# Constant matmuls into spare score columns where the planner sees TensorE idle, with new keys for the first part

## The chip, the cores and the metric

The kernel runs on one core of a Trainium2 chip. The metric is the time of one execution on the device in microseconds (us). Before the change the median of three runs is 1089.22 us (1087.53 to 1090.05). The profile is of one further execution, whose own time is 1085.3 us; its span, from the first to the last instruction, is 1083.5 us.

## What is computed

Attention over 4 batches, 8 heads, 576 positions and a head width of 64, in which each row keeps only the scores within `tau` of its maximum, then two feed-forward layers of 2304 tokens, width 512 and hidden width 2048:

```python
scores = scale * np.matmul(q, k.transpose(0, 1, 3, 2))
thresh = np.max(scores, axis=-1, keepdims=True) - tau
scores = np.where(scores >= thresh, scores, -1000000000.0)
scores = scores - np.max(scores, axis=-1, keepdims=True)
attn = np.exp(scores)
attn = attn / (np.sum(attn, axis=-1, keepdims=True) + 1e-09)
x = np.matmul(attn, v)                  # heads joined: 2304 x 512
h = x @ w_in;  x = (h * np.clip(h + 3.0, 0.0, 6.0) / 6.0) @ w_out
h = x @ w2_in; x = (h - np.tanh(h)) @ w2_out
```

## The kernel before

**Numbers in pairs.** To keep float32 accuracy on TensorE (PE), operands are split into a high and a low part and multiplied in three passes (`mm3`, L502). The weights arrive as 64-bit values and are put together by shifts and masks on VectorE (DVE; L432, L435, L438).

**Units of attention.** `units` lists 144 units, each one block of 128 queries of one head (or the left-over queries of two heads). `softmax(u)` makes the scores of a unit on PE (L692: four matmuls of 288 columns, or eight for the left-over queries, 640 in all) into a PSUM tile `s` of two banks, of which each uses 288 of its 512 columns (`ps.t[:, :, 0:SH]`). Three readers follow: the maximum on DVE (L697), the exponential on ScalarE (ACT, L699), and on DVE the comparison with the threshold, multiplied by the exponential (L708). There are two such tiles (`R_s`), so unit u+2 waits for L708 of unit u. The weights of attention are then split (L713 on ACT, L719 on GpSimd, POOL), transposed by a DMA (`pt`), and multiplied with the values (`products`, L745, 28 matmuls of 65 columns for each block).

**The first feed-forward layer** has two halves of the hidden width and eight blocks of tokens. Ten passes (`PASSES`, `layer1`) run beside attention: 12 matmuls of `m<-xT,wo` (L502) for each of 8 hidden tiles, 96 in a pass, and 96 of `m<-g,wo` (L933). Six more passes (`ENDING`) follow, and then the second layer. Its weights need a scale first (`weights_done`: L995 on PE, L1000 to L1016 on DVE), and each block of tokens too (`x_scale`, `x_round`: L482, L489, L827 on PE, L832 on DVE).

**What sets the order.** All work is recorded as tasks by `plan.add(eng, dur, key, fn, ...)`: an engine, a duration, a key, what is read and written. `Plan.issue` then runs a list schedule by these durations: whenever an engine is free, the ready task with the lowest key is issued, and `fn` emits its instructions. So the order of every engine's queue is fixed at build time; on the chip each engine takes its queue in order, and semaphores hold it where a partner is late. The constants `LK, LQ, ...` (how many units ahead keys and queries are transposed), `T0, W0, FO, FW` (when attention, weights and passes are due) and `PVK, GK, RK` (offsets of keys) set the keys. The durations are those of a full TensorE clock: 0.53 us for a unit's scores, 0.404 us for a block's products.

Of the kernel before, what the change touches and what calls it, by code (L numbers as in the profile page):

```python
# [2 lines left out]

# [11 lines left out]
BF16 = mybir.dt.bfloat16  # L15
# [57 lines left out]
class Plan:  # L73
# [8 lines left out]
    SAME = {"pe": 0.0, "act": 0.1, "dve": 0.127, "pool": 0.03, "dma": 0.0, None: 0.0}  # L82

    def __init__(self):
        self.tasks = []

    def add(self, eng, dur, key, fn, r=(), w=(), after=(), xfer=0.0, hold=False, slack=0.0, port=None):
        r, w = ([getattr(b, "of", b) for b in x] for x in (r, w))
# [14 lines left out]
    def issue(self):  # L103
        succ = {t: [] for t in self.tasks}
        left = {}
        for n, t in enumerate(self.tasks):
            t.seq = n
            for b in t.w:
                t.deps.update(dict.fromkeys(b.ring.after))
                if b.prev is not None:  # L110
                    t.deps.update(dict.fromkeys(b.prev.users))
            t.deps.pop(t, None)
            left[t] = len(t.deps)
            for d in t.deps:
                succ[d].append(t)
        engs = ("pe", "act", "dve", "pool", "dma", None)
        free = dict.fromkeys(engs, 0.0)
        pending = {e: [] for e in engs}
        avail = {e: [] for e in engs}
        at = dict.fromkeys(self.tasks, 0.0)  # L120
        for t in self.tasks:
            if not left[t]:
                heapq.heappush(pending[t.eng], (0.0, t.seq, t))
        rings = {b.ring for t in self.tasks for b in t.free}
        slacks = {t.slack for t in self.tasks}
        now, done, moving = 0.0, 0, 0.0
        port = {"dve": 0.0, "pool": 0.0}
        while done < len(self.tasks):
            for e in engs:
                while pending[e] and pending[e][0][0] <= now:  # L130
                    t = heapq.heappop(pending[e])[2]
                    heapq.heappush(avail[e], (t.key, t.seq, t))
                if free[e] > now:
                    continue
                held = []
                while avail[e]:
                    x = heapq.heappop(avail[e])
                    if all(b.slot is not None or b.ring.slot_at(now - x[2].slack) is not None for b in x[2].free):
                        break
                    held.append(x)  # L140
                    x = None
                else:
                    x = None
                for y in held:
                    heapq.heappush(avail[e], y)
                if x is None:
                    continue
                t = x[2]
                for b in t.free:
                    if b.slot is None:  # L150
                        b.slot = b.ring.slot_at(now - t.slack)
                        b.ring.slots[b.slot] = float("inf")
                t.fn()
                t.start = now
                done += 1
                end = free[e] = (max(now, port["pool" if e == "dve" else "dve"]) if t.port else now) + t.dur
                if t.port:
                    port[e] = end
                if t.xfer or e == "dma":
                    end = moving = max(moving, now + 1.3) + t.xfer  # L160
                    if t.hold:
                        free[e] = max(free[e], end - 0.9)
# [12 lines left out]
            nxt = [x + y for r in rings for x in r.slots for y in slacks if now < x + y < float("inf")]  # L175
            for e in engs:
                if free[e] > now and (avail[e] or pending[e]):
                    nxt.append(free[e])
                elif pending[e]:
                    nxt.append(pending[e][0][0])  # L180
            nxt = [x for x in nxt if x > now]
            assert nxt or done == len(self.tasks), "the tasks wait for each other"
            if nxt:
                now = min(nxt)
        return now
# [15 lines left out]
def attention_moe_moe_kernel(  # L201
# [29 lines left out]
    nc = tc.nc  # L231
# [3 lines left out]
    KD = DM // 128  # L235
    FH = DFF // 2
    MH = FH // 128
# [5 lines left out]
    SH = S // 2  # L243
# [11 lines left out]
    plan = Plan()  # L255
# [1 line left out]

    LAG = 4
    STEP, SLOW, KNEE = 3.0, 0.8, 4
    LK, LQ, LV, LD = 5, 3, 1, 4  # L260
    XL, FO = 1, 7
    FW = 38.0
    W0, WS, WO = 8.0, 0.8, -2.0
    PVK, GK, RK = -4.0, -6.0, -1.0
    T2O = 0.0
    PASSES = [(0, 0, 0), (0, 1, 0), (1, 0, 0), (0, 0, 1), (1, 1, 0), (0, 1, 1), (2, 0, 0), (1, 0, 1), (2, 1, 0), (3, 0, 0)]
    CLAMP, LOD = True, (8, 8)
# [4 lines left out]
    F0, EK, CL, P2L, CF = 2.0, 4.0, 0.2, 22.0, 1.0  # L272
    NF, SF, PACE, PREP, PW, TK = 18, 14, 11.0, 2, 55.0, 40
    PK, PREP0 = (100.0, 90.0), 1
    T0 = 12.0
    WB0, WBS, WBD, WBL, WBP = 34, 2, 0.8, 8.0, 3.0
    WAL, WAP = 7.0, 0.8
    ZU, TAIL = 30, 3
    ST, SB, CS = 4.0, 2.0, 0.0


    const = ctx.enter_context(tc.tile_pool(name="const", bufs=1))
# [193 lines left out]
            out=p.bitcast(I32), in0=p.bitcast(I32), scalar1=0x7F800000, scalar2=None, op0=ALU.bitwise_and)  # L476
        nc.vector.reciprocal(out=inv, in_=p)

    def highest(src, top, key, after, ring):

        bank = ring.new()
        x = add("pe", 0.3, key, lambda: nc.tensor.transpose(bank.t[0:1, 0:128], src, ident), w=[bank], after=after)  # L482
        return add("dve", 0.26, key + 0.1, lambda: nc.vector.tensor_reduce(
            out=top, in_=bank.t[0:1, 0:128], axis=AX.X, op=ALU.max), r=[bank], w=[bank], after=[x])

    def everywhere(top, key, after, ring, dur, fn):

        bank = ring.new()
        x = add("pe", 0.1, key + 0.2, lambda: nc.tensor.matmul(  # L489
            bank.t[:, 0:1], ones[0:1, :], top, start=True, stop=True), w=[bank], after=after)  # L490
        return add("dve", dur, key + 0.3, lambda: fn(bank.t[:, 0:1]), r=[bank], w=[bank], after=[x])

    def flat(ap):
# [167 lines left out]
    def queries(b, g, j, h, c, part):  # L661

        if c == NC:
            return QT[b, "l", j].t[:, part, h % 2 * LF:h % 2 * LF + 2 * LF]
        return QT[b, g, j].t[:, part, h % 2, c % 2 * 128:c % 2 * 128 + 128]

    GT, XT = {}, {}

    def sum_group(u):

# [5 lines left out]
    def softmax(u, key):  # L676
# [9 lines left out]
        ex = lambda: e.t[:, n, :].rearrange("p (a s) -> p a s", a=2)  # L686

        def scores():
            ops = [(queries(b, g, j, x, c, part), KS[b, j].t[:, x % 2]) for x in hs for part in range(2)]
            for i, (l, ks) in enumerate(ops):  # L690
                for half in range(2):
                    nc.tensor.matmul(  # L692
                        ps.t[:, half, 0:SH], l, ks[:, half * SH:(half + 1) * SH], start=i == 0, stop=i == len(ops) - 1,
                    )
# [96 lines left out]
    def x_scale(b, g, key):  # L791

        hb = 2 * b + g
        x = add("dve", 0.15, key, lambda: nc.vector.tensor_reduce(
            out=xtop[:, hb:hb + 1], in_=xsq[:, hb, 0:2 + g], axis=AX.X, op=ALU.max), after=x_done[b, g])
        x = highest(xtop[:, hb:hb + 1], one[0:1, hb % 4:hb % 4 + 1], key + 0.1, [x], R_tp)
        x = everywhere(one[0:1, hb % 4:hb % 4 + 1], key + 0.1, [x], R_tp, 0.45, lambda bank: root(
            bank, xpow[:, 0, hb:hb + 1], xpow[:, 1, hb:hb + 1]))
        x_scaled[b, g] = x

    def x_unscale(b, g, half, key):
# [11 lines left out]
    def x_round(b, g, i, key):  # L813
# [12 lines left out]
            for kk in range(KD):  # L826
                nc.tensor.transpose(pv()[:, kk, :], xn()[:, kk * 128:(kk + 1) * 128], ident[0:w, 0:w])  # L827

        add("pe", 0.00085 * KD * w, key, tr, r=[xt], w=[tp, xT], after=[x_scaled[b, g]])
        hi = add("act", t_act(KD * w, scalars=True), key + RK, lambda: nc.scalar.activation(  # L830
            out=xT.t[:, 0, :, cols], in_=pv(), func=ACTF.Copy, scale=s), r=[tp], w=[xT])
        add("dve", t_dve(KD * w, scalars=True), key + RK, lambda: nc.vector.scalar_tensor_tensor(  # L832
# [107 lines left out]
        turn.append(last)  # L940

    with tc.manual_schedule():
        make_identity(nc, ident)
        nc.sync.dma_start(out=tau_b[:, 0:1], in_=tau.partition_broadcast(128))
        nc.vector.tensor_scalar(out=tau_b[:, 1:2], in0=tau_b[:, 0:1], scalar1=0.0, scalar2=None, op0=ALU.max)
# [2 lines left out]
        )  # L948
        nc.vector.tensor_scalar(out=tau_b[:, 3:4], in0=tau_b[:, 1:2], scalar1=-1.0, scalar2=None, op0=ALU.mult)
        nc.vector.memset(three[:, 0:1], 3.0 * GS)  # L950
        nc.vector.memset(ones, 64.0)
        nc.vector.memset(xsq.rearrange("p b i -> p (b i)"), 0.0)
        for t in vt_t:
            for i in range(2):
                nc.gpsimd.memset(t[:, i, :, :, D:D + 1].rearrange("p h c d -> p (h c) d"), 1.0 - i)
# [28 lines left out]
        def weights_done(half, kind, key, step):  # L984
# [12 lines left out]
            x = add("pe", 0.07 * MH * KD, key, norms, r=ss, w=[gram], after=w_found[half, kind])  # L997
# [5 lines left out]
            x = add("dve", 0.5, key, diagonal, r=[gram], w=[gram], after=[x])  # L1003
            bank = R_tp.new()
            x = add("pe", 0.12, key, lambda: nc.tensor.matmul(
                bank.t[:, 0:1], ones, top, start=True, stop=True), w=[bank], after=[x])
# [135 lines left out]
        key = T2  # L1142
# [451 lines left out]
```

## Time and profile before

| | us |
|---|---|
| median of three runs | 1089.22 |
| profiled execution, its own time | 1085.3 |
| its span | 1083.5 |
| PE busy (92% of the span) | 996.8 |
| DVE busy (75%) | 813.5 |
| ACT busy (67%) | 724.5 |
| POOL busy (33%) | 354.7 |

The page cuts the span into 40 slices of 27 us and gives the busy share of each engine in tenths, and the clock that TensorE was granted. A busy share says little by itself; what a stage waits for is read from the views of waits and from the chain of work that ended last, in windows of the stage in question.

### The profile page before, as it was taken

The page shows a single profiled execution, that of the slowest core. Times are in us where ns is not written, and L with a number is a line of the kernel's source. Part 1 is how long each engine was busy: PE and PEld are TensorE (multiplying, and loading weights), DVE is VectorE, ACT ScalarE, POOL GpSimd, SP SyncE. Part 2 cuts the span into 40 slices and gives each one's busy share as a digit, 9 for nine tenths or more (in the row PEclk, how much of TensorE's full clock was granted, in tenths as well). Part 3 has the DMA queues.
Part 4 walks back from the last instruction along what each step waited for, and adds up shares of the span by engine and source line. Part 5 has one row for each costly group of instructions (what it writes and reads, how often), then busy time and mean ns, then how long its engine had stood idle before and what let it go on. Part 6 is the DMA issues. An engine that isn't in the chain of part 4 may idle for free.

```text
span 1083.5 us, 23225 instructions
## 1 busy us (share of the span) xinstructions
PE 996.8 (92%) x8919; PEld 762.9 (70%) x8919; DVE 813.5 (75%) x1625; ACT 724.5 (67%) x1347; POOL 354.7 (33%) x377
## 2 busy tenths in 40 slices
PE   5654987989899999999999999999999999999998
PEld 4553776768788788888786787876576666666664
DVE  5888888979687587877557894478987796784664
ACT  6775877888998688876645874457756675574332
POOL 3553545776775565764310000000001111111000
PEclk8686997999999999999999999999999999999999
DMA  7896689988778667667468744224334866574235
GB/s 185 177 203 173 136 177 209 194 198 158 141 159 170 123 155 171 115 146 159 92 198 266 262 154 121 64 85 139 100 126 124 200 136 115 127 127 51 87 96 138
DMA packets 284943, 161.43 MB, mean 149 GB/s; under 512 B 203168, under 2 KB 261024, under 8 KB 284832
## 3 DMA queue, kind: packets, MB, share of 16 engines
q1 hardware_dynamic: 279024, 150.25, 56.8%
q0 software_dynamic: 5184, 9.44, 6.4%
q8 instruction: 70, 1.15, 0.4%
q14 instruction: 41, 0.34, 0.1%
q10 hardware_dynamic: 624, 0.26, 0.1%
HBM read 76.02 MB, written 41.42 MB: 108 GB/s over the span
## 4 chain that ended last, share of the span: by engine, by line
PE 73%; DVE 10%; ACT 8%; DMA 4%; issue 3%; POOL 1%; SPq 0%; ACTq 0%; DVEq 0%
PE ya L502 23%; PE m L502 19%; PE h L502 9%; PE m L933 7%; PE s L692 6%; PE tp L745 5%; DMA pt<-pp 2%; DVE e L708 2%; PE tp L575 2%; ACT e L699 1%; DMA xT<-xs 1%; DVE z L697 1%; DVE m L435 1%; DVE wo L438 1%; PE tp L827 1%
## 5 line engine op out<-in xcount | busy, mean ns | idle before, releaser
L502 PEld LDWEIGHTS <-wo 128*128 128x128 f16 x2112 | 201.5, 98 | 59.1 <-issue 4.6
L719 POOL TENSOR_TENSOR pp<-e,pp 128x128 f16<-128x128 f32 (+3 forms) x156 | 180.3, 1176 | 115.1 <-ACT pp L713 67.7
L502 PE MATMUL ya<-wo,g 128*128 128x512 f16 x864 | 205.4, 379 | 2.5 <-DVE g L857 1.3
L502 PEld LDWEIGHTS <-wi 128*128 128x128 f16 x1536 | 150.0, 98 | 39.3
L502 PE MATMUL m<-xT,wo 128*128 128x256 f16 (+1 forms) x1248 | 171.8, 286 | 3.9 <-DVE wo L438 3.2
L1414 POOL DMA_DIRECT2D po<-o x36 | 31.3, 876 | 410.5 <-ACT o L1408 410.5
L502 PEld LDWEIGHTS <-g 128*128 128x128 f16 x864 | 83.7, 98 | 82.1 <-DVE g L857 3.1
L708 DVE SCALAR_TENSOR_TENSOR e<-s,z,e 128x576 f32<-128x576 f32 x144 | 116.4, 812 | 30.6 <-ACT e L699 26.5
L933 PE MATMUL m<-g,wo 128*128 128x256 f16 (+1 forms) x960 | 129.4, 284 | 5.3 <-ACT y L878 2.7
L697 DVE TENSOR_REDUCE z<-s 128x1 f32<-128x576 f32 x144 | 107.6, 752 | 34.1 <-PE s L692 33.2
L692 PE MATMUL s<-ks,q 128*128 128x288 f32 x512 | 107.8, 338 | 22.5 <-DVE e L708 20.0
L853 ACT ACTIVATE g<-t 128x512 f16<-128x512 f32 (+1 forms) x168 | 94.8, 565 | 45.9 <-DVE t L1381 24.8
L699 ACT ACTIVATE e<-s,z 128x576 f32<-128x576 f32 x144 | 105.4, 737 | 26.4 <-DVE z L697 20.8
L933 PEld LDWEIGHTS <-wo 128*128 128x128 f16 x960 | 90.3, 98 | 27.7 <-issue 5.5
L692 PEld LDWEIGHTS s<-ks,q 128*128 128x128 f32 x512 | 80.2, 207 | 30.3 <-issue 16.0
L502 PE MATMUL m<-x,wi 128*128 128x256 f16 x768 | 94.9, 273 | 0.0
L745 PE MATMUL tp<-vt,pt 128*128 128x65 f16 (+1 forms) x2240 | 89.3, 200 | 5.5 <-DMA pt<-pp 2.7
L745 PEld LDWEIGHTS <-pt 128*128 128x128 f16 (+1 forms) x2240 | 83.5, 105 | 14.2 <-issue 6.8
L1379 ACT ACTIVATE t<-t,hid_s 128x512 f32<-128x512 f32 x72 | 51.6, 718 | 62.6 <-DVE t L1370 62.0
L713 ACT ACTIVATE pp<-e 128x1152 f16<-128x1152 f32 (+1 forms) x80 | 85.1, 1064 | 10.0 <-DVE e L708 5.5
L502 PE MATMUL ya<-g,wo 128*128 128x320 f16 (+1 forms) x576 | 78.0, 290 | 0.4 <-DVE g L860 0.4
L845 ACT ACTIVATE t<-m,three,unscale 128x320 f32<-128x320 f32 (+1 forms) x76 | 51.2, 674 | 40.1 <-PE m L502 39.8
(164 smaller groups left out, 1560.8 us busy)
## 6 DMA issues: line engine op xcount, KB each, us to landing
st<-in_moe_w_in_dram SPq DMA_DIRECT2D x32, 512.0 KB, 4.7
st<-in_moe_w_out_dram SPq DMA_DIRECT2D x32, 512.0 KB, 4.6
po<-o POOLq DMA_DIRECT2D x36, 256.0 KB, 4.4
ys<-y SPq DMA_DIRECT2D x32, 160.0 KB, 1.8
y<-ys SPq DMA_DIRECT2D x9, 512.0 KB, 6.2
po<-o SPq DMA_DIRECT2D x18, 256.0 KB, 2.0
o<-po SPq DMA_DIRECT2D x18, 256.0 KB, 3.2
kr<-in_k_dram SPq DMA_DIRECT2D x16, 256.0 KB, 3.7
```

Of the source, the lines that this page charges most:

```text
L502: nc.tensor.matmul(ps, l[a], r[b], start=first and t == 0 and i == 0, stop=last and t == 2 and i == n - 1,)
L692: nc.tensor.matmul(ps.t[:, half, 0:SH], l, ks[:, half * SH:(half + 1) * SH], start=i == 0, stop=i == len(ops) - 1,)
L697: add("dve", 0.69, key, lambda: nc.vector.tensor_reduce(out=z.t[:, 0:1], in_=s(), axis=AX.XY, op=ALU.max, negate=True), r=[ps], w=[z])
L699: exp = add("act", 0.66, key, lambda: nc.scalar.activation(out=ex(), in_=s(), func=ACTF.Exp, bias=z.t[:, 0:1]), r=[ps, z], w=[e])
L708: add("dve", 0.74, key, lambda: nc.vector.scalar_tensor_tensor(out=ex(), in0=s(), scalar=z.t[:, 1:2], in1=ex(), op0=ALU.is_ge, op1=ALU.mul ...
L713: high = add("act", t_act(w * S, sbuf=True), key, lambda: nc.scalar.activation(out=pp.t[:, 0:w, 0:S], in_=e.t[:, 0:w, :], func=ACTF.Copy), ...
L719: add(eng, dur, key, lambda src=src, dst=dst, queue=queue: queue.tensor_tensor(out=pp.t[:, 0:w, dst], in0=e.t[:, 0:w, src], in1=pp.t[:, 0: ...
L745: nc.tensor.matmul(pv.t[0:m, w_ * (D + 1):(w_ + 1) * (D + 1)], pt.t[:, n, blk, rows], vv, start=o == 0, stop=o == len(ops) - 1)
L845: add("act", t_act(n, scalars=True) + 0.05, key, lambda: nc.scalar.activation(out=t(), in_=ps(), func=ACTF.Relu, bias=three[:, 0:1], scale ...
L853: hi = add("act", t_act(n, sbuf=True), key, lambda: nc.scalar.activation(out=gh(), in_=t(), func=ACTF.Copy, scale=GS2 if far else 1.0), r= ...
L933: prev = [add("pe", t_half(n, 1), kd, lambda o=o, l=l, r=r, m=m, s=s, ps=ps, gt=gs[m // 2]: nc.tensor.matmul(ps.t[:, 0:n], W1[half, "o", m ...
L1379: add("act", t_act(2 * NB, sbuf=True, scalars=True), key, lambda: nc.scalar.activation(out=s_(), in_=h.t, func=ACTF.Tanh, scale=c), r=[h], ...
```

## The change

While `Plan.issue` finds no ready task for PE before 470 us of the plan's own time, it looks at how much of the last 3.4 us PE has worked in the plan; below a share of 0.55 it issues a filler: two matmuls of a constant tile (`ones`) of 224 columns each into columns 288 to 511 of the two banks of the score tile that was written last. Nothing reads those columns. 24 such matmuls stand ahead of everything, and the memset of `ones` moves to the head of DVE's queue. Filling ends with the scores of the last unit. Twelve of the constants that set keys and leads are changed; the three new `LG, LX, LR` are zero, so their `slack` arguments change nothing.

```diff
+        worked = deque()
...
+                if x is None and e == "pe" and self.idle is not None and now < self.until:
+                    low = now - 3.4
+                    while worked and worked[0][1] <= low:
+                        worked.popleft()
+                    if sum(z - max(y, low) for y, z in worked) < self.share * 3.4:
+                        x = (0.0, 0, Task("pe", 0.19, 0.0, self.idle, {}, 0.0, False, 0.0, False))
+                        x[2].free, succ[x[2]] = [], []
+                        self.tasks.append(x[2])
...
+                if e == "pe":
+                    worked.append((now, end))
...
-    LK, LQ, LV, LD = 5, 3, 1, 4
-    XL, FO = 1, 7
-    FW = 38.0
-    W0, WS, WO = 8.0, 0.8, -2.0
-    PVK, GK, RK = -4.0, -6.0, -1.0
+    LK, LQ, LV, LD = 5, 2, 1, 4
+    XL, FO = 1, 6.1
+    FW = 35.6
+    W0, WS, WO = 7.2, 0.8, -2.0
+    PVK, GK, RK = -7.0, -5.0, -2.6
...
-    T0 = 12.0
-    WB0, WBS, WBD, WBL, WBP = 34, 2, 0.8, 8.0, 3.0
-    WAL, WAP = 7.0, 0.8
+    T0 = 10.2
+    WB0, WBS, WBD, WBL, WBP = 34, 2, 0.8, 6.1, 3.0
+    WAL, WAP = 7.0, 1.82
...
-    ST, SB, CS = 4.0, 2.0, 0.0
+    ST, SB, CS = 5.3, 2.9, 0.0
+    SHARE, UNTIL, FIRST_FILL = 0.55, 470.0, 24
+    LG, LX, LR = 0.0, 0.0, 0.0
...
+    scored = [None]
+
+    def filler(n=2):
+
+        spare = scored[0].t[:, :, SH:512]
+        for i in range(n):
+            nc.tensor.matmul(
+                spare[:, i % 2], ones.bitcast(BF16)[:, 0:128], ones.bitcast(BF16)[:, 0:512 - SH], start=True, stop=True)
...
         def scores():
+            scored[0] = ps
+            if u == NU - 1:
+                plan.until = 0.0
...
+        nc.vector.memset(ones, 64.0)
         make_identity(nc, ident)
...
-        nc.vector.memset(ones, 64.0)
         nc.vector.memset(xsq.rearrange("p b i -> p (b i)"), 0.0)
+        plan.idle, plan.until, plan.share = filler, UNTIL, SHARE
+        ps0 = R_s.new()
+
+        def first():
+            scored[0] = ps0
+            filler(FIRST_FILL)
+
+        add("pe", 0.19 * FIRST_FILL, -100.0, first, w=[ps0])
```

The changed kernel has 374 filler matmuls, each with its load of weights, in 50 runs of 2 to 34. All other counts on PE are as before. In the rows below a line number is one of the kernel named; L717, L722, L724, L733 of the changed kernel are L692, L697, L699, L708 of the one before, L516 is L502, L958 is L933, L770 is L745, L589 is L575, L605 is L591, L656 is L642.

PE's queue at the start, first of the kernel before (`kr` and `qr` are raw keys and queries, `left` those of the last 64 positions, `tp` a PSUM bank for transposes):

```order
L575 MATMUL tp<-ident,kr 128x128 [waits DMAHW3_49,Pool_49]
L575 MATMUL tp<-ident,kr 128x128 x3
L575 MATMUL tp<-ident,qr 128x128 [waits DMAHW0_49,Pool_49]
...
L591 MATMUL tp<-ident,left 64x64 [waits DMAHW4_49,DVE_49,PE_49]
...
L642 MATMUL tp<-vs,ones 128x1 [waits DVE_49]
L692 MATMUL s<-ks,q 128x288
L692 MATMUL s<-ks,q 128x288 [waits Activation_49]
```

and of the changed kernel:

```order
L688 LDWEIGHTS ones [waits DVE_49]
L688 MATMUL s<-ones 128x224
...
L589 MATMUL tp<-ident,kr 128x128 [waits DMAHW3_49,Pool_49]
L589 MATMUL tp<-ident,kr 128x128 x3
L605 MATMUL tp<-ident,left 64x64 [waits DMAHW4_49]
...
L589 MATMUL tp<-ident,qr 128x128 [waits DVE_49,DMAHW0_49,PE_49,Pool_49]
...
L656 MATMUL tp<-vs,ones 128x1 [waits DVE_49,Activation_49]
...
L717 MATMUL s<-ks,q 128x288 [waits Activation_49]
```

24 fillers stand ahead of the first transposes, 6 ahead of the queries' and 8 behind `vs`, and the second pair of heads' keys is transposed ahead of the first scores.

PE's queue of the changed kernel behind the scores of units 0 and 1, where the first fillers stand that wait:

```order
L656 MATMUL tp<-vs,ones 128x1 [waits DVE_49,PE_49,Activation_49]
L688 LDWEIGHTS ones
L688 MATMUL s<-ones 128x224 [waits DVE_49]
...
L688 MATMUL s<-ones 128x224 [waits Activation_49]
...
L605 MATMUL tp<-ident,left 64x64 [waits DVE_49]
```

and DVE's queue there, the readers of the same tiles:

```order
L722 TENSOR_REDUCE z<-s 128x1 [waits PE_49]
...
L733 SCALAR_TENSOR_TENSOR e<-s,z,e 128x576 [waits Activation_49]
L621 SCALAR_TENSOR_TENSOR q<-tp,tau_b,q 128x512 [waits Activation_49]
L733 SCALAR_TENSOR_TENSOR e<-s,z,e 128x576 [waits PE_49]
L722 TENSOR_REDUCE z<-s 128x1 [waits PE_49]
```

Four fillers wait for DVE's maximum, four more for ACT's exponential, and the second L733 now waits for PE, which L708 never did in the kernel before. In the whole program 11 fillers wait for DVE and 16 for ACT, 12 of the L733 wait for PE, and 12 of the L724 wait for PE where 4 of the L699 did. Behind a wait for DVE stand 60 fillers in the same runs, and behind a wait for ACT 70.

PE's queue around the last unit's scores, first of the kernel before:

```order
L745 LDWEIGHTS pt
L745 MATMUL tp<-vt_160,pt 64x65
L692 MATMUL s<-ks,qs_163 128x288 [waits DVE_49,PE_49]
L692 MATMUL s<-ks,qs_163 128x288 x7
L502 LDWEIGHTS wo
L502 MATMUL m<-xT,wo 128x320 [waits PE_49]
```

and of the changed kernel:

```order
L958 LDWEIGHTS wo
L958 MATMUL m<-g_8814,wo 128x320
L717 MATMUL s<-ks,qs_163 128x288 [waits DVE_49,PE_49]
L717 MATMUL s<-ks,qs_163 128x288 x7
L958 LDWEIGHTS wo
L958 MATMUL m<-g_8487,wo 128x320 [waits Activation_49]
```

Ahead of the last unit's scores the kernel before has issued 816 matmuls of L502 and 768 of L933, in the first half of its ninth pass; the changed kernel has issued 864 of L516 and 816 of L958, and is halfway through the ninth pass's outputs. The first matmul of the first pass stands behind 104 score matmuls before, and behind 120 now.

## Rows read from the trace of the kernel before

**Rows 1.** The page: busy time (share) xinstructions of each engine, then 40 slices of 27 us.

```profile
PE 996.8 (92%) x8919; PEld 762.9 (70%) x8919; DVE 813.5 (75%) x1625; ACT 724.5 (67%) x1347; POOL 354.7 (33%) x377
...
PE   5654987989899999999999999999999999999998
...
DVE  5888888979687587877557894478987796784664
...
PEclk8686997999999999999999999999999999999999
```

**Rows 2.** Busy time in three stretches: us, each engine (x count), clock, DMA, GB/s.

```profile
0.00:190.00 190.00, 128.66 (x1267) 109.99 (x1268) 158.85 (x298) 139.30 (x261) 94.82 (x114) 0.80 0.81 180
190.00:610.00 420.00, 402.09 (x4372) 332.20 (x4370) 317.05 (x673) 321.55 (x609) 228.66 (x228) 1.00 0.75 165
610.00:1083.50 473.50, 466.06 (x3284) 320.66 (x3282) 337.56 (x657) 263.67 (x478) 31.26 (x36) 1.00 0.47 122
```

**Rows 3.** The same columns for eleven stretches in the first 190 us (first three, eighth, sum).

```profile
0.00:14.30 14.30, 6.99 (x30) 5.84 (x30) 4.74 (x17) 6.86 (x12) 1.89 (x16) 1.00 0.78 211
17.70:34.80 17.10, 12.50 (x65) 9.72 (x64) 15.29 (x26) 15.95 (x31) 9.85 (x11) 0.50 0.63 140
38.20:48.40 10.20, 7.81 (x64) 6.96 (x61) 7.58 (x16) 8.97 (x18) 7.51 (x7) 0.50 0.99 206
...
96.20:109.90 13.70, 4.91 (x46) 3.53 (x44) 12.86 (x19) 7.18 (x13) 4.63 (x6) 0.50 0.32 93
...
sum 89.50, PE 62.02 PEld 52.80 DVE 68.48 ACT 59.01 POOL 42.28; mean PE 5.64 PEld 4.80 DVE 6.23 ACT 5.36 POOL 3.84
```

**Rows 4.** Timeline of PE: start us, us, what. Half clock first, then full clock.

```profile
20.48 1.30 PE L692 MATMUL s<-ks,q 128*128 128x288 f32 x4 [0.95 <-DVE e L708]
...
301.04 0.78 PE L692 MATMUL s<-ks,q 128*128 128x288 f32 x4
```

**Rows 5.** Waits in 0 to 190 us: who waited for whom: us, times, longest.

```profile
PE s L692 <- DVE e L708: 18.3, 14, 2.5
DVE z L697 <- PE s L692: 13.0, 16, 3.0
...
PE tp L827 <- DVE xT L832: 8.0, 2, 7.2
PE tp L995 <- DVE ks L600: 6.0, 1, 6.0
```

**Rows 6.** Chain of work, pieces of PE: start us, us, what, x matmuls.

```profile
108.11 1.71 PE m L502 x8
...
256.71 2.62 PE m L502 x24
...
566.96 1.63 PE m L502 x12
```

**Rows 7.** Groups by line and shape, 0 to 250 us: x count | busy us, mean ns.

```profile
L708 DVE SCALAR_TENSOR_TENSOR e<-s,z,e 128x576 f32<-128x576 f32 x62 | 50.0, 812 | 6.9 <-ACT e L699 4.1 <-ACT z L702 2.2
L697 DVE TENSOR_REDUCE z<-s 128x1 f32<-128x576 f32 x64 | 47.7, 752 | 14.9 <-PE s L692 14.7
L699 ACT ACTIVATE e<-s,z 128x576 f32<-128x576 f32 x62 | 45.4, 738 | 13.3 <-DVE z L697 10.3 <-POOL pp L719 1.2 <-DVE rl L772 1.0
```

**Rows 8.** Timeline of the start, DVE and PE.

```profile
3.80 0.15 DVE L945 TENSOR_SCALAR tau_b<-tau_b 128x1 f32<-128x1 f32 x1 [3.80 <-DMA tau_b<-in_tau_dram]
...
4.13 0.17 DVE L951 MEMSET ones<- 128x128 f32 x1
...
5.07 1.09 PE L575 MATMUL tp<-ident,kr 128*128 128x128 f32 x4 [5.07 <-DMA kr<-in_k_dram]
...
10.44 1.31 PE L692 MATMUL s<-ks,q 128*128 128x288 f32 x4
```

**Rows 9.** PE's waits in 190 to 610 us, the three longest.

```profile
PE tp L745 <- DMA pt<-pp: 2.7, 3, 1.2
PE m L933 <- ACT y L878: 2.7, 2, 1.8
PE s L692 <- DVE e L708: 2.1, 5, 0.6
```

**Rows 10.** Busy time ahead of two falls of the clock (columns as in rows 2).

```profile
34.80:38.20 3.40, 1.91 (x34) 1.63 (x32) 3.33 (x9) 1.72 (x6) 1.58 (x2) 1.00 0.76 201
161.10:167.90 6.80, 3.87 (x51) 2.99 (x48) 6.16 (x13) 5.63 (x13) 5.49 (x6) 1.00 1.20 213
167.90:174.70 6.80, 5.99 (x67) 5.72 (x68) 6.47 (x15) 5.14 (x10) 5.51 (x6) 0.50 0.76 169
```

More of the change, by code (lines that the diff above doesn't have):

```diff
@@ L1 @@
 import heapq
+from collections import deque
 from contextlib import ExitStack
@@ L84, in __init__ @@
     def __init__(self):
-        self.tasks = []
+        self.tasks, self.idle = [], None
     def add(self, eng, dur, key, fn, r=(), w=(), after=(), xfer=0.0, hold=False, slack=0.0, port=None):
@@ L176, in issue @@
             for e in engs:
-                if free[e] > now and (avail[e] or pending[e]):
+                if free[e] > now and (avail[e] or pending[e] or e == "pe" and now < self.until):
                     nxt.append(free[e])
@@ L477, in power, with highest, everywhere @@
         nc.vector.reciprocal(out=inv, in_=p)
-    def highest(src, top, key, after, ring):
+    def highest(src, top, key, after, ring, slack=0.0):
         bank = ring.new()
-        x = add("pe", 0.3, key, lambda: nc.tensor.transpose(bank.t[0:1, 0:128], src, ident), w=[bank], after=after)
+        x = add("pe", 0.3, key, lambda: nc.tensor.transpose(bank.t[0:1, 0:128], src, ident), w=[bank], after=after, slack=slack)
         return add("dve", 0.26, key + 0.1, lambda: nc.vector.tensor_reduce(
             out=top, in_=bank.t[0:1, 0:128], axis=AX.X, op=ALU.max), r=[bank], w=[bank], after=[x])
-    def everywhere(top, key, after, ring, dur, fn):
+    def everywhere(top, key, after, ring, dur, fn, slack=0.0):
         bank = ring.new()
         x = add("pe", 0.1, key + 0.2, lambda: nc.tensor.matmul(
-            bank.t[:, 0:1], ones[0:1, :], top, start=True, stop=True), w=[bank], after=after)
+            bank.t[:, 0:1], ones[0:1, :], top, start=True, stop=True), w=[bank], after=after, slack=slack)
         return add("dve", dur, key + 0.3, lambda: fn(bank.t[:, 0:1]), r=[bank], w=[bank], after=[x])
@@ L795, in x_scale @@
             out=xtop[:, hb:hb + 1], in_=xsq[:, hb, 0:2 + g], axis=AX.X, op=ALU.max), after=x_done[b, g])
-        x = highest(xtop[:, hb:hb + 1], one[0:1, hb % 4:hb % 4 + 1], key + 0.1, [x], R_tp)
+        x = highest(xtop[:, hb:hb + 1], one[0:1, hb % 4:hb % 4 + 1], key + 0.1, [x], R_tp, LX)
         x = everywhere(one[0:1, hb % 4:hb % 4 + 1], key + 0.1, [x], R_tp, 0.45, lambda bank: root(
-            bank, xpow[:, 0, hb:hb + 1], xpow[:, 1, hb:hb + 1]))
+            bank, xpow[:, 0, hb:hb + 1], xpow[:, 1, hb:hb + 1]), LX)
         x_scaled[b, g] = x
@@ L827, in tr @@
                 nc.tensor.transpose(pv()[:, kk, :], xn()[:, kk * 128:(kk + 1) * 128], ident[0:w, 0:w])
-        add("pe", 0.00085 * KD * w, key, tr, r=[xt], w=[tp, xT], after=[x_scaled[b, g]])
+        add("pe", 0.00085 * KD * w, key, tr, r=[xt], w=[tp, xT], after=[x_scaled[b, g]], slack=LR)
         hi = add("act", t_act(KD * w, scalars=True), key + RK, lambda: nc.scalar.activation(
@@ L995, in norms @@
                         nc.tensor.matmul(gram.t[:, 0:128], part, part, start=x + c == 0, stop=x == MH - 1 and c == KD - 1)
-            x = add("pe", 0.07 * MH * KD, key, norms, r=ss, w=[gram], after=w_found[half, kind])
+            x = add("pe", 0.07 * MH * KD, key, norms, r=ss, w=[gram], after=w_found[half, kind], slack=LG)
             def diagonal():
@@ L1005, in weights_done @@
             x = add("pe", 0.12, key, lambda: nc.tensor.matmul(
-                bank.t[:, 0:1], ones, top, start=True, stop=True), w=[bank], after=[x])
+                bank.t[:, 0:1], ones, top, start=True, stop=True), w=[bank], after=[x], slack=LX)
             ready = w_scaled[half, kind] = add("dve", 0.45, key, lambda: root(
```

## The prediction

> **What bounds the kernel now.** I read the page first: PE is busy 996.8 us of a span of 1083.5 us, so all of PE's idle time together is 86.7 us [rows 1]. The slices show where it lies: from the twelfth on PE stands at 9 to the end, but for the last slice, and in the first eight it stands at 4 to 9 while DVE stands at 8 or 9 from the second on. The clock line is below 9 in five of the first seven slices and at 9 ever after. Three stretches [rows 2] put numbers to it: to 190 us PE is busy 128.66 us of 190 (61.3 us idle) and DVE 158.85 us; from 190 to 610 us PE is busy 402.09 of 420 (17.9 us idle); behind that PE idles 7.4 us. So behind 190 us the kernel is PE's work, and a change can only take from the 17.9 us or have had more of the work done before. Ahead of 190 us it is a relay between DVE and PE in which DVE is nearer to its limit: the waits [rows 5] show PE's scores standing 18.3 us for DVE's L708 to free their tile, and DVE's maximum L697 standing 13.0 us, 16 times, for scores.
>
> The third view is the clock. In eleven stretches of the first 190 us [rows 3] the granted clock is 0.50, half of 2.4 GHz (the first stretch has no record of it, and the column then says 1.00, but its four score matmuls take 1.31 us [rows 8], as those at 0.50 do). They are 89.5 us long, and PE is busy 62.02 us in them. One unit's scores take 1.30 us there and 0.78 us at full clock [rows 4], so half the clock costs a unit 0.52 us.
>
> **The change, part by part.**
>
> *Clock.* If fillers kept the clock full throughout, the 62.02 us would take half, and PE would be busy 31.0 us less. That is one bound. The other is 0: the reader is to see that DVE is busy 158.85 of 190 us, and where PE then waits for L708 a faster matmul only waits longer. A loss is excluded, since a faster matmul delays nobody. Between them I go by the row that says when DVE waited for PE: 16 waits for scores at 0.52 us less each are 8.3 us, and they can't give more than their 13.0 us. I take **-8.3 us**. Shorter transposes are left in the upper bound.
>
> *The fillers' own time.* A matmul of 256 columns takes 1.71 us / 8 = 0.214 us at half clock and 2.62 / 24 = 0.109 us at full [rows 6]; scaled to 224 columns that is, as an estimate, 0.187 and 0.096 us. 374 of them are 36 us at full clock. All stand ahead of the 292nd of 640 score matmuls, where PE idles 61.3 us up to 190 us and some more behind; so the time is there, and I cost it at nothing where a filler only fills. If that cover were gone (PE late against the plan, so that fillers stand ahead of work that is ready), the whole 36 us would be added, less the clock's gain.
>
> The first 24 cost 4.5 us at half clock. They wait for `ones`, whose memset moves from 4.13 us, behind the wait for tau that ended at 3.80 [rows 8], to the head of DVE's queue. From about 0.8 us on they would end near 5.3 us; the first transposes began at 5.07 us when their keys had landed. That is 0.2 to 0.3 us late, which I count below. DVE's other steps there, and the number of DMAs on SP, ACT and POOL, do not change; leads only shift which load stands ahead of which.
>
> *The ties.* The order shows what the diff does not: although nothing reads the spare columns, 27 fillers wait for a reader of the same tile (11 for DVE, 16 for ACT), and 12 of the L733 and 12 of the L724 wait for PE. A maximum takes 752 ns, an exponential 738, a thresholded product 812 [rows 7]. What is queued behind a waiting filler is PE's next real work; in nearly every run that instruction waits for DVE or a DMA itself, so blocking PE costs little. The readers are dearer: behind a wait for the maximum stand fillers that the exponential waits for, behind the exponential those that L733 waits for. 60 + 70 = 130 fillers stand in such places, 12.5 us at 0.096. Below, the cost is 0, if PE is through before the reader is due; above it is 27 waits of 0.75 us, 20 us. DVE works through 158.85 of 190 us and mostly has other work ahead of the waiting reader, so a third of the 12.5 is nearest: **+4 us**, with the late start in it.
>
> The Trainium skill (PSUM — Partial Sum Buffer, section "PSUM bank collisions raise a hardware error") asks for semaphores by bank and partition quadrant and not by address, because two engines in different columns of one bank still collide; the waits in the order agree with that rule, no run here shows a collision, and by it "unused" columns are only free while no reader of the score bank is open, which would put the ties nearer to their upper end, 20 us, and the sum at 1091.
>
> *Keys and leads.* Twelve constants change, so every queue is shuffled. At the last unit's scores the changed kernel has issued 48 more matmuls of L502's kind and 48 of L933's, of 320 columns; at 1.63 / 12 = 0.136 us [rows 6] these are 13 us of PE's work that stand ahead of attention's end rather than behind it. It pays only where it fills idle time. PE idles 17.9 us between 190 and 610 us, in short waits for transposed weights, for a bank that ACT empties, for L708 [rows 9]; with more of the first layer's work within reach they can shrink, at most to 0. The other bound: attention itself may end 13 us later and its tail be exposed, a loss of as much. In the first part the first pass starts 16 score matmuls later (behind 120, not 104), with DVE's weight steps spread wider, the place where PE now stands 7.2 us for `xT` [rows 5]. I take a third of the idle, **-6 us**, since each of the three longest kinds of wait is under 3 us and no single one can be taken away whole.
>
> *Sum.* 1085.3 - 8.3 + 4 - 6 = 1075.0 us against the profiled execution. The median of the runs stands 3.9 us above that execution (1089.22), so the forecast for the median is **1079 us**, 0.9% faster.
>
> **Rivals.**
>
> *The ties decide (slower).* Place: the readers L733 and L724 of the first 60 units. Each unit's maximum, exponential and product become a chain with fillers between them. Price: the 130 tied fillers wholly on the path, 12.5 us, with handovers and the 0.3 us at the start some 13 us; the interrupted fill leaves the clock half its gain, -4; attention is then later, so the keys give nothing. 1089.2 + 13 - 4 = **1098 us**. It decides once the ties cost more than clock and keys give. For it: the planner that placed the fillers doesn't know these waits. Against it: DVE's other work covers, and in 14 places PE waited for L708 anyway.
>
> *The clock does not hold (no change).* The planner stops filling as soon as PE has worked 0.55 of its recent time, counted by full-clock durations, transposes among them. In the trace the clock fell at 38.2 us [rows 3] after PE had worked 1.91 of 3.4 us, and at 167.9 us after 3.87 of 6.8 us [rows 10], so partly busy stretches precede falls. If most of the eleven stretches stay, the clock gives some -2, the tied fillers cost double, +8, and the keys -6: **1089 us**. Speaking for it, the Trainium skill (TensorE: Matmul & The Clock Gate, section "Part 4: PE-mode transpose") says that transposes don't count as the engine's activity as other matmuls do; by that rule the planner would stop too early wherever transposes made up its share. Agreeing with it is the first stretch, half transposes and at half clock throughout, though it was also thinly filled.
>
> *DVE hides the clock's gain.* The clock stays full, but PE then only waits longer for L708 (18.3 us already): clock 0, ties +2, keys -6, so **1085 us**, with PE's waits for L708 grown by what its matmuls lost.
>
> **How the numbers follow.** Chances: forecast 0.48, ties 0.20, clock not held 0.17, DVE hides it 0.15. A measurement of this kernel can tell some 0.2%, 2.2 us, from no change, so faster ends at 1087.0 and slower begins at 1091.4. Faster: 0.46 of the forecast, 0.10 of the last rival, 0.05 of the clock's, 0.01 of the ties', 0.62. Same: 0.01, 0.04, 0.08, 0.03 in that order, 0.16. Slower: 0.01, 0.01, 0.04, 0.16, 0.22. The range begins where the clock gives its whole 13.0 us, the keys two thirds of the idle (12) and the ties cost 2: 1089.2 - 23 = 1066. It ends at 1097, just within the ties' rival; under the low end lies 0.08, over the high end 0.10.
>
> **What would show it.** Clock: over 0.93 in the first 190 us where it was 0.80, scores near 0.78 us there, and DVE's waits for scores well under 13.0 us. Ties: new waits of fillers (L688) for L722 or L724, of some 0.7 us each, and L733 or L724 waiting for L688, under 5 us in sum. Keys: PE's idle time from 190 to 610 us near 12 us, not 17.9. I am wrong if the clock rises and the last unit's scores still come no earlier relative to PE's work, if waits for L688 pass 12 us, or if the clock stays at half in more than a third of the 89.5 us.

## The result and the profile after

The changed kernel runs in 1079.9 us (median of four runs, 1077.62 to 1080.13), the kernel before, on the same chip, in 1088.9 us: a ratio of 0.9913, with a 95% interval of 0.9895 to 0.9931. It is faster by 0.9%. Measured again on another chip in the course of the experiments the ratio was 0.9953 (0.9939 to 0.9967), so faster by 0.5 to 0.9%; the forecast, 1079 us or 0.9%, stands at the upper end of that. Its three terms do not hold, as the experiments show: the ties cost more and the order gives more than forecast, and the clock, as far as the runs can tell, gives less.

The page after, its lines on the span, the engines, PE's slices and the clock ([rows 1] before):

```profile
span 1077.9 us, 24007 instructions
...
PE 1016.5 (94%) x9293; PEld 780.7 (72%) x9293; DVE 808.4 (75%) x1625; ACT 723.9 (67%) x1347; POOL 355.2 (33%) x377
...
PE   7667996999999999999999999999999999999998
...
PEclk9998999999999999999999999999999999999999
```

PE is busy 1016.5 us, 20 more than before, and the span is still 5.6 us shorter: PE's idle time fell from 86.7 to 61.4 us, most of that filled rather than removed. The clock line, which went 8686997 before, now goes 9998. The same three stretches as in [rows 2], with the third cut at this kernel's end:

```profile
0.00:190.00 190.00, 144.51 (x1584) 124.36 (x1585) 157.47 (x294) 137.09 (x257) 93.17 (x111) 0.96 0.79 176
190.00:610.00 420.00, 411.08 (x4472) 340.19 (x4469) 311.64 (x667) 323.59 (x611) 230.77 (x230) 1.00 0.73 165
610.00:1078.00 468.00, 460.89 (x3245) 316.17 (x3243) 339.33 (x665) 263.24 (x481) 31.26 (x36) 1.00 0.48 126
```

The mean clock of the first 190 us rose from 0.80 to 0.96, while DVE did no more work in them (157.47 us against 158.85). From 190 to 610 us PE idles 8.9 us where it idled 17.9. The waits of the first 190 us ([rows 5] before) have new names:

```profile
PE s L688 <- ACT e L724: 15.0, 14, 1.9
...
PE s L688 <- DVE z L722: 10.6, 10, 2.0
...
ACT e L724 <- PE s L688: 8.7, 8, 2.4
...
DVE e L733 <- PE s L688: 4.4, 5, 2.0
...
DVE z L722 <- PE s L717: 3.7, 5, 1.6
...
DVE z L722 <- PE s L688: 3.2, 7, 0.7
...
PE s L717 <- DVE e L733: 2.8, 4, 1.3
```

PE's scores no longer wait 18.3 us for L733 (the old L708) but 2.8. In their place the fillers, L688, stand 15.0 us for the exponential and 10.6 us for the maximum; and the readers wait for fillers: the exponential 8.7 us, the product 4.4, the maximum 3.2, together 16.3. DVE's maximum waits 3.7 us for scores in place of 13.0, but maximum and product now stand 7.6 us for fillers. The timeline of PE shows the place whose order stands ahead of the prediction:

```profile
17.34 0.54 PE L688 MATMUL s<-ones 128*128 128x224 bf16 x4 [0.34 <-DVE z L722]
18.71 0.54 PE L688 MATMUL s<-ones 128*128 128x224 bf16 x4 [0.83 <-ACT e L724]
...
20.32 0.77 PE L717 MATMUL s<-ks,q 128*128 128x288 f32 x4
```

Four fillers start when the maximum has ended, four more when the exponential has, and the scores behind them follow. The chain of work in these 190 us names the fillers first, with 15.1%:

```profile
by line: PE s L688 15.1%; DVE z L722 9.5%; ACT e L724 7.4%; PE s L717 6.5%; issue 6.3%; ACT wo L1047 4.6%; PE tp L770 4.6%; DVE ks L614 4.2%; DMA pt<-pp 3.4%; PE m L958 3.2%; PE m L516 3.2%; DVE m L449 2.9%; DVE e L733 2.9%; PE tp L589 2.8%
```

### The profile page after: what moved, and what is told of

Same layout as the page of the kernel before. It is cut to its first block, busy times and chain, and to the rows that moved or that the text cites. A ratio compares the mean times of both kernels' runs of the same rounds, so it can differ in the third digit from the quotient of the medians.

```text
span 1077.9 us, 24007 instructions
## 1 busy us (share of the span) xinstructions
PE 1016.5 (94%) x9293; PEld 780.7 (72%) x9293; DVE 808.4 (75%) x1625; ACT 723.9 (67%) x1347; POOL 355.2 (33%) x377
## 4 chain that ended last, share of the span: by engine, by line
PE 79%; DVE 9%; ACT 6%; DMA 3%; issue 2%; POOL 1%; SPq 0%; ACTq 0%; DVEq 0%
PE ya L516 23%; PE m L516 22%; PE h L516 9%; PE m L958 8%; PE s L717 6%; PE tp L770 5%; PE s L688 3%; DVE z L722 2%; PE tp L589 2%; ACT e L724 2%; DMA pt<-pp 2%; DVE e L733 1%; DVE ks L614 1%; ACT wo L1047 1%; DVE m L449 1%
## 5 line engine op out<-in xcount | busy, mean ns | idle before, releaser
L516 PEld LDWEIGHTS <-wo 128*128 128x128 f16 x2112 | 201.2, 98 | 57.4 <-issue 1.7
L516 PE MATMUL ya<-wo,g 128*128 128x512 f16 x864 | 205.4, 379 | 2.5 <-DVE g L882 1.3
L516 PEld LDWEIGHTS <-wi 128*128 128x128 f16 x1536 | 149.7, 98 | 39.6
L516 PE MATMUL m<-xT,wo 128*128 128x256 f16 (+1 forms) x1248 | 168.8, 285 | 2.5 <-DVE t L872 1.5
L516 PEld LDWEIGHTS <-g 128*128 128x128 f16 x864 | 83.5, 98 | 82.3 <-DVE g L882 3.1
L733 DVE SCALAR_TENSOR_TENSOR e<-s,z,e 128x576 f32<-128x576 f32 x144 | 116.5, 812 | 29.0 <-ACT e L724 19.6
L722 DVE TENSOR_REDUCE z<-s 128x1 f32<-128x576 f32 x144 | 107.7, 751 | 35.4 <-PE s L717 31.6
L958 PE MATMUL m<-g,wo 128*128 128x256 f16 (+1 forms) x960 | 128.7, 284 | 1.3 <-ACT y L903 0.6
L724 ACT ACTIVATE e<-s,z 128x576 f32<-128x576 f32 x144 | 105.6, 737 | 30.9 <-DVE z L722 19.1
L958 PEld LDWEIGHTS <-wo 128*128 128x128 f16 x960 | 89.3, 98 | 22.9 <-issue 1.8
L717 PE MATMUL s<-ks,q 128*128 128x288 f32 x512 | 101.3, 322 | 4.0 <-DVE e L733 3.7
L738 ACT ACTIVATE pp<-e 128x1152 f16<-128x1152 f32 (+1 forms) x80 | 85.0, 1062 | 15.9 <-DVE e L733 15.1
L516 PE MATMUL m<-x,wi 128*128 128x256 f16 x768 | 94.9, 273 | 0.0
L770 PE MATMUL tp<-vt,pt 128*128 128x65 f16 (+1 forms) x2240 | 83.4, 195 | 10.0 <-ACT x L777 2.9
L770 PEld LDWEIGHTS <-pt 128*128 128x128 f16 (+1 forms) x2240 | 78.5, 101 | 18.4 <-issue 13.0
L717 PEld LDWEIGHTS s<-ks,q 128*128 128x128 f32 x512 | 74.6, 193 | 10.0 <-DVE e L733 5.8
L688 PE MATMUL s<-ones 128*128 128x224 bf16 x374 | 52.4, 283 | 26.9 <-ACT e L724 15.0
L516 PE MATMUL ya<-g,wo 128*128 128x320 f16 (+1 forms) x576 | 77.5, 290 | 0.0
```

Of the source, the lines that this page charges most:

```text
L516: nc.tensor.matmul(ps, l[a], r[b], start=first and t == 0 and i == 0, stop=last and t == 2 and i == n - 1,)
L688: nc.tensor.matmul(spare[:, i % 2], ones.bitcast(BF16)[:, 0:128], ones.bitcast(BF16)[:, 0:512 - SH], start=True, stop=True)
L717: nc.tensor.matmul(ps.t[:, half, 0:SH], l, ks[:, half * SH:(half + 1) * SH], start=i == 0, stop=i == len(ops) - 1,)
L722: add("dve", 0.69, key, lambda: nc.vector.tensor_reduce(out=z.t[:, 0:1], in_=s(), axis=AX.XY, op=ALU.max, negate=True), r=[ps], w=[z])
L724: exp = add("act", 0.66, key, lambda: nc.scalar.activation(out=ex(), in_=s(), func=ACTF.Exp, bias=z.t[:, 0:1]), r=[ps, z], w=[e])
L733: add("dve", 0.74, key, lambda: nc.vector.scalar_tensor_tensor(out=ex(), in0=s(), scalar=z.t[:, 1:2], in1=ex(), op0=ALU.is_ge, op1=ALU.mul ...
```

## The experiments

Each kernel was timed in five rounds against the kernel before. Ratios are to that, with 95% intervals.

**The order without the fillers.** The body of the filler is emptied; the planner still reserves its places, so every engine's queue is the changed kernel's, less the fillers.

```diff
     def filler(n=2):
...
-        spare = scored[0].t[:, :, SH:512]
-        for i in range(n):
-            nc.tensor.matmul(
...
+        return
```

> The changed kernel with every engine's order unchanged, but the 374 fillers emit nothing (their places in the plan stay). Clock theory (the prediction's: clock -8.3, ties +4, keys -6): the clock falls back to about 0.80 in the first 190 us, and the time is some 4 us above the changed kernel, 1084, a little under the kernel before. Rival, the order alone did it: no slower than the changed kernel's 1079.9, or some 4 us faster as the ties are gone, 1076.

Measured: 1075.59 us, ratio 0.9889 (0.9871 to 0.9906), against 1087.7 us of the kernel before. The clock fell back, and the kernel got faster than the change. The two intervals overlap, so both kernels were run again on one chip.

> The order alone once more (fillers emit nothing), on the same chip. Fillers cost something: ratio near 0.989, 1075 to 1076, at a mean clock near 0.96. Fillers cost nothing: within 1.5 us of the changed kernel.

> The changed kernel once more, on one chip with the order alone, since their ratios to the kernel before (0.9913 and 0.9889) have intervals that overlap. If the fillers cost what the medians say: 4 us above the order alone, ratio near 0.991. If the two are one: a difference under 1.5 us.

Measured: order alone 1076.14 us, ratio 0.9891 (0.9875 to 0.9908); the changed kernel 1082.81 us, ratio 0.9953 (0.9939 to 0.9967); the kernel before 1088.07 us. So the order is worth 12 us, all of the gain and more, and the fillers cost 6.7 us net on that chip (some 3 us by the ratios of the first measurement). The order alone, two stretches of the second of these profiles:

```profile
0.00:190.00 190.00, 138.81 (x1287) 119.18 (x1288) 159.23 (x303) 141.30 (x265) 95.74 (x114) 0.78 0.82 181
190.00:610.00 420.00, 409.79 (x4432) 338.65 (x4431) 312.79 (x675) 324.04 (x612) 227.52 (x228) 1.00 0.73 166
```

Its clock in the first 190 us is 0.78, below that of the kernel before, and PE idles 51.2 us there in place of 61.3, and 10.2 us from 190 to 610 us in place of 17.9. Two stretches hold 9.9 of these some 18 us. First the kernel before, then the order alone:

```profile
80.00:108.00 28.00, 10.83 (x114) 9.72 (x115) 25.09 (x46) 15.46 (x30) 11.89 (x15) 0.67 0.68 177
215.00:315.00 100.00, 89.52 (x1062) 76.47 (x1062) 79.87 (x175) 87.49 (x161) 73.60 (x73) 1.00 0.82 165
```

```profile
80.00:108.00 28.00, 17.10 (x157) 14.23 (x156) 25.18 (x49) 19.86 (x41) 14.03 (x19) 0.68 0.77 196
215.00:315.00 100.00, 93.11 (x1079) 80.03 (x1077) 81.25 (x172) 91.23 (x166) 73.11 (x74) 1.00 0.77 163
```

From 80 to 108 us, where the first weights and the first tokens get their scales, PE worked 10.83 us and now works 17.10; from 215 to 315 us it idles 6.9 us in place of 10.5. The waits of the order alone in the first 190 us say what left and what came:

```profile
PE s L714 <- DVE e L730: 19.4, 15, 2.7
PE tp L767 <- DVE ks L614: 6.2, 3, 2.6
PE tp L767 <- ACT x L774: 5.9, 2, 3.5
...
PE tp L849 <- DVE xpow L475: 1.5, 1, 1.5
...
PE tp L849 <- DVE xT L854: 1.2, 1, 1.2
```

The token's transposes (L849, the old L827), which stood 8.0 us for `xT` and 3.1 us for its scale before, now stand 1.2 and 1.5; the 6.0 us in which the weights' sums (the old L995) stood behind DVE are gone. New are the waits of the products (L767, the old L745), 6.2 us for DVE and 5.9 us for ACT, which before had stood 1.6 and 0.5 us for DVE and not for ACT. PE's wait for the score tile, 19.4 us, is as long as it was (18.3).

**The fillers without the order.** The kernel before, its planner watching for idle time and emitting fillers without reserving any time for them; every other instruction stands where it stood, but for the memset of `ones`, which moves to the front.

```diff
+                    if e == "pe" and self.idle is not None and filled <= now < self.until:
...
+                            self.idle()
+                            filled = now + 0.19
+                            worked.append((now, filled))
                     continue
```

> The kernel before with every engine's order unchanged (only the memset of ones moves to the front), 24 fillers at the start and 396 more where its own plan leaves TensorE idle. They take no time in the plan, so nothing is displaced. Clock theory: clock above 0.93 in the first 190 us, and 1088.9 - 8.3 + 4, about 1084.6. Rival, order alone: 1089 to 1093 in spite of a full clock, as DVE hides it and the ties cost.

Measured: 1088.64 us (twelve runs), ratio 1.0013 (0.9998 to 1.0028): no change, at a clock that is as full as forecast. The stretch to 190 us, and from its waits those of the fillers (L690) and of the readers (L735 is the old L708, L726 the old L699):

```profile
0.00:190.00 190.00, 152.37 (x1643) 130.57 (x1644) 157.26 (x295) 138.33 (x259) 93.92 (x112) 0.94 0.81 178
```

```profile
PE s L690 <- ACT e L726: 9.7, 10, 1.5
...
PE s L690 <- DVE z L724: 7.1, 11, 1.2
...
DVE e L735 <- PE s L690: 3.4, 6, 1.4
...
ACT e L726 <- PE s L690: 2.2, 2, 1.4
```

This is the counterpart of the order alone: 0.80 to 0.94 in the clock, nothing in the time. It is a net, since these fillers are tied too: they stand 16.8 us for readers, and readers 5.6 us for them. A gain of the clock and a price of the ties may stand against each other here; the 4.3 us less that -8.3 + 4 asked for are not there.

**The ties taken away.** In the changed kernel's order a filler goes only into a score tile of which no reader is open in the plan, and is left out otherwise.

```diff
+        ok = [x for x in (scored[0], scored[1]) if x is not None and not getattr(x, "till", 0.0) > plan.now]
+        if not ok:
+            return
-        spare = scored[0].t[:, :, SH:512]
+        spare = ok[0].t[:, :, SH:512]
```

> The changed kernel with its order unchanged, but a filler is only emitted into a score tile of which, in the plan, no reader is open; 222 of 374 fillers are left and none of them waits for DVE or ACT. If the ties cost 4 us: 1076. If the 25 us that fillers stood waiting were free: 1080. If fewer fillers let the clock fall again in a third of the stretches: 1082 to 1083.

Measured: 1075.38 us, ratio 0.9884 (0.9868 to 0.99): the order alone again, with 222 fillers on the engine and the clock at 0.87.

```profile
0.00:190.00 190.00, 143.96 (x1484) 124.25 (x1484) 160.90 (x303) 141.41 (x265) 96.86 (x114) 0.87 0.81 183
```

```profile
PE s L721 <- DVE e L733: 20.1, 15, 2.3
...
DVE z L729 <- PE s L692: 5.9, 8, 1.5
```

Freed from the ties, the fillers and the better clock together change nothing: PE stands 20.1 us for L733, and the maximum stands 5.9 us for fillers ahead of it. That neither of the two is worth anything is not shown; over the whole span the clocks are close, 0.975 on average in these four runs and 0.966 in the five of the order alone. With one matmul in place of two (111 fillers):

> The untied fillers of before, one matmul in place of two: 111 fillers (12 at the start), none of which waits, order unchanged. If the clock is worth some 5 us (wide fillers against narrow ones with the same ties gave 4.9) and the untied 222 gave back as much by holding up maxima (5.9 us of DVE's waits for fillers): half the hold-up, 1072 to 1073, if the clock stays near 0.87. If the clock falls to the 0.77 of the order alone, or is worth nothing without ties: 1075.5.

Measured: 1079.05 us, ratio 0.9907 (0.9881 to 0.9933), with runs from 1071.89 to 1081.28 and a mean clock no higher than the order's own. No gain; whether it is a loss of 3 us or none is left open.

**The ties without the activity.** All 374 fillers and all their waits, of 8 columns in place of 224.

```diff
-        spare = scored[0].t[:, :, SH:512]
+        spare = scored[0].t[:, :, SH:SH + 8]
```

> The changed kernel with its order and all 374 fillers and their waits unchanged, but each of 8 columns in place of 224: the ties without most of the fillers' activity, so that the clock should fall back to the 0.77 that the order alone has in the first 190 us. If the ties cost by waiting, some 22 us (give and take): up to 1097, over 1085 at any rate. If they cost 4 us: 1080. If what costs is the length of the fillers and not the waits: 1076 to 1078.

Measured: 1084.81 us, ratio 0.9969 (0.9955 to 0.9983), 8.7 us above the order alone.

```profile
0.00:190.00 190.00, 144.21 (x1566) 127.15 (x1567) 155.76 (x289) 134.61 (x255) 92.53 (x111) 0.76 0.78 174
```

```profile
PE s L688 <- ACT e L724: 12.9, 12, 2.0
...
PE s L688 <- DVE z L722: 8.0, 8, 2.4
...
ACT e L724 <- PE s L688: 5.6, 6, 1.7
```

The clock is 0.76, as without fillers, and fillers stand 20.9 us for readers. The 8.7 us are the price of the waits with little of the fillers' own time: at the start 24 narrow fillers take 0.80 us, 0.033 us each, where a wide one takes an estimated 0.096 us at full clock. The time is just below the 1085 us of the first reading. Wide fillers at a clock of 0.96 cost 3 to 7 us although each is longer: where fillers stand in the chain, a fuller clock gives back 2 to 6 us, and more by what the length costs.

**Doubled and halved.** Four matmuls in a filler in place of two, or one.

```diff
-        for i in range(n):
+        for i in range(2 * n):
```

> The changed kernel with its order unchanged and every filler of four matmuls in place of two, the first 48 in place of 24: 748 fillers. Both the time of the fillers and the length of the tied runs double. If ties cost 4 us by the length of their runs: some 4 us more and 4.5 us at the start, 1084 to 1088. If ties cost by the wait and not by the length, and the clock is full already: under 1082.

Measured: 1102.33 us, ratio 1.013 (1.0112 to 1.0147): 19 to 24 us above the change by the ratios, where 4 to 8 were expected.

```profile
0.00:190.00 190.00, 157.09 (x1749) 140.76 (x1750) 140.02 (x258) 123.71 (x231) 85.93 (x103) 0.97 0.70 159
```

```profile
DVE e L733 <- PE s L688: 13.4, 7, 4.2
...
ACT e L724 <- PE s L688: 11.5, 7, 3.7
...
DVE z L722 <- PE s L688: 7.9, 8, 2.4
```

The clock hardly rose, from 0.96 to 0.97. The readers now stand 32.8 us for fillers where they stood 16.3, and DVE gets through 140.02 us of work in 190, 17 less. The 130 tied fillers more are 12.5 us at full clock, and the readers' waits grew by 16.5: the length of a tied run counts, and by more than a third. All fillers were doubled at once, so what the others add to the 19 to 24 us is not separated.

> The changed kernel with its order unchanged and every filler of one matmul in place of two (187 in all, 12 at the start); the 27 waits of fillers stay. From the order alone (1075.6) to the change (1079.9) to doubled fillers (1102.3) two readings are open. Give and take: 374 fillers cost some 22 us and the full clock gives some 18; half of them cost 11, and if the clock holds the time is 1075.6 + 11 - 18, near 1069, and if it holds by half, 1078. Hidden clock: the clock gives nothing, DVE hides it, and fillers cost 4 us as they stand; then half cost 2: 1077 to 1078 whatever the clock does.

Measured: 1078.97 us, ratio 0.9914 (0.9898 to 0.9931), the same as the change; its mean clock in the runs lies between the change's and the order's. It rules out the 1069 of give and take with a clock that holds. Give and take with a clock that holds by half (1078; the profile has 0.90 in the first 190 us) and the hidden clock (1077 to 1078) both come near, so this run does not decide between them.

**The first 24.** The first fillers left out, the rest kept.

> The changed kernel without its first 24 fillers (their place in the plan stays), 350 are left. The first unit's maximum starts at 15.4 us in the changed kernel and at 14.4 in the order alone, so if that delay is carried through: 1.0 us less, 1079. If a full clock from the start is worth more than the delay: 1080 to 1082. Either way the bulk of the cost of the ties stays, so not under 1077.

Measured: 1084.04 us, ratio 0.9962 (0.9947 to 0.9977). Against the change's 0.9913 this would be a loss of 5 us, against its 0.9953 none, so what the first fillers are worth is not settled.

**What made the order.** The new constants with a planner that knows no fillers; and the old constants with the fillers' places reserved and left empty.

> The twelve new constants alone: the planner runs without any filler, neither in its plan nor on the engine, so the order is set anew. If the gain of the order lies in the constants: about 1075.6. If it lies in the one order that constants and filler places gave together: nearer to the kernel before, 1084 to 1094.

> The old constants with the fillers' places in the plan, which emit nothing on the engine: the other half of what set the order. If the gain of the order lies in the constants: no gain, 1088 or more. If holding TensorE for fillers in the plan makes a better order by itself: under 1085.

Measured: 1099.31 us, ratio 1.0099 (1.0081 to 1.0118), and 1092.55 us, ratio 1.0039 (1.0022 to 1.0055). Each half by itself is slower than the kernel before. The gain lies in the one order that the constants and the places gave together. What in that order is worth it is read from the waits above; no run changes one part of it by itself.

## Why the prediction was right in the number and wrong in its terms

**Clock, -8.3 us: the step that failed.** The step put 16 waits of DVE for scores, shortened by 0.52 us each, on the path. Every sign that I asked of the clock came: the clock rose (0.96, over 0.93), scores take 0.77 us, and DVE's waits for scores fell from 13.0 to 3.7 us. The time did not follow: in the old order the fillers gave 0.94 and 1.4 us more (from 0.2 less to 3.0 more), where 4.3 less was forecast with the ties. A check that needs no edit bounds the clock by itself: over the 56 runs of the kernel before that stand beside these experiments, the mean granted clock varied between 0.953 and 0.978; 22 runs at 0.958 or less have a median of 1088.1 us, 8 runs at 0.969 or more 1088.0. A straight line through all 56 falls by 0.55 us for 0.01 of clock (95%: between a fall of 1.3 and a rise of 0.2). From the profile's 0.965 to 1.00 that is, as an estimate, 2 us and at most 4.4, so the term was some four times too large for the kernel before.

Why so much of it is lost is argued and not shown. DVE waiting for scores and PE waiting for L708 are two sides of one relay, so a faster score may only wait longer for its tile, which was the rival "DVE hides the clock's gain" (0.15). But that rival's sign, PE's wait for L708 grown, did not come: it is 20.1 us with untied fillers at a clock of 0.87, and 20.5 and 19.4 us in the two profiles of the order alone at 0.77 and 0.78; where tied fillers stand in between, it shrank (2.8 us in the change).

Nor do the runs say that the clock is worth nothing in every order. Of the nine runs of the order alone, without any filler, the two at a mean clock of 0.974 and 0.976 took 1074.05 and 1073.84 us, the seven at 0.956 to 0.962 took 1074.79 to 1077.73. Of the twelve runs of the old order with fillers, the four at 0.988 or more took 1086.35 to 1087.83 us, the four at 0.984 or less 1089.63 to 1093.62. These are differences between runs, and what else differed in them is not known.

**Ties, +4 us: right in kind, too small.** The waits read from the order are there, 25.6 us of PE's, and the readers' 16.3 us are past the 12 us at which I said I would be wrong (L733 and L724 alone stand 13.1 us, where under 5 was asked for). They cost 8.7 us with narrow fillers, and 3 to 7 us with wide ones, net of what the clock gives back. The Trainium skill's rule (PSUM — Partial Sum Buffer, "PSUM bank collisions raise a hardware error"), to guard a bank and not an address, is what these waits do, and its direction was right; the 1091 us beside it stand against the profiled execution and are 1095 against the median, as the forecast is. I took a third of the tied fillers' time because DVE mostly had other work; the doubled fillers, with which DVE does 17 us less in 190, speak against that.

**Keys and leads, -6 us: right in sign for the order, half of its size, and not by the keys alone.** The order alone gives 12 us, but the twelve constants by themselves cost some 11 (1099.31 against 1088.26 us). The places reserved for fillers, whose part in the order I did not price, belong to the gain, though by themselves they cost some 4 (1092.55). PE's idle time from 190 to 610 us fell by 7.7 us, near the 6 forecast. What I left out is the first 190 us, where it fell by 10.1 us: [rows 5] showed 8.0 and 6.0 us in which PE stood in the stage of the first scales (the 3.1 I had not read), and I named the place but took no gain from it. The 13 us of moved work can be followed at the last unit's scores, here of the kernel before, the order alone and the change:

```profile
518.08 1.32 PE L692 MATMUL s<-ks,qs 128*128 128x288 f32 x8
```

```profile
522.20 1.32 PE L714 MATMUL s<-ks,qs 128*128 128x288 f32 x8
```

```profile
527.56 1.32 PE L717 MATMUL s<-ks,qs 128*128 128x288 f32 x8
```

From there to the end of the span it is 565.4, 550.8 and 550.3 us. In the order alone 13 us more of PE's work stand ahead of these scores, which start only 4.1 us later, and 14.6 us less stand behind them. In the change they start 5.4 us later still, and no more is saved behind: what the fillers cost lies ahead of the last scores.

**The sum.** -8.3 + 4 - 6 is -10.3 us. Measured it is about -12 for the order and +3 to +7 for the fillers, clock and ties together. For clock and ties I had forecast -4.3, so that was wrong by 7 to 11 us, and the order by 6 the other way. That the sum hit was luck.

**Rivals.** Ties did not decide, as the order gave more than I allowed it; with fillers doubled they do. The clock held, so the rule in the Trainium skill that transposes count less as activity (TensorE: Matmul & The Clock Gate, Part 4) did not show here as lost clock; no run isolates it.

The fastest version is the order without fillers, 1075.6 and 1076.1 us, 1.1% under the kernel before and 6.7 us under the change on one chip. Untied fillers equal it and add nothing that can be measured.

## What to carry to other kernels

When a change adds instructions through a scheduler, run its order with the added instructions silent: here the order was all of the gain and the instructions cost part of it. Columns that nobody reads are not free if their bank is guarded as a whole: count the waits that the order shows on both sides, the readers' above all. And before paying for a faster clock, see whether the engine that it speeds up is waiting on the path: run-to-run differences of the clock in the kernel as it is may bound its worth at no cost, for that order and not for another.

## What the runs showed that I had not expected

The kernel before took the same time at a mean clock of 0.953 to 0.958 as at 0.969 to 0.978, while the order alone ran faster in the two runs in which its clock was higher. And 222 fillers with no ties, some 21 us of PE's time at 0.096 us each, left the time where it was (1075.38 against 1075.59 us), at a clock of 0.87 in place of 0.77 in the first 190 us, though the engine is busy 94% of the span.
